# Linear attention and a ReLU MLP on one core: denominators computed per head, their reciprocals repeated through DRAM, and key sums on VectorE

## The chip, the cores and the metric

The kernel runs on one core of one Trainium2 chip. A core has five engines that run side by side and are held together by semaphores: TensorE (in the profile PE, with its weight loads as PEld), VectorE (DVE), ScalarE (ACT), GpSimd (POOL) and SyncE (SP), which here issues all DMA transfers. Operands lie in SBUF, a memory of 128 partitions; matmul results go to PSUM, eight banks of 128 x 512 fp32 values. The metric is the time of one execution on the device, in microseconds, as the median over runs.

## The reference

The input is x with 2048 rows of 512 bf16 values. The block is a linear attention with 32 heads of 16 values, followed by an MLP of width 1792, both behind a layer norm and a residual.

```
def _layernorm(x): return (x - mean(x)) / sqrt(var(x) + 1e-5)

def _A_ref(x, wqkv, wo):                     # H = 32, Dh = 16
    q, k, v = (x @ wqkv) split in three, by heads
    phi = lambda t: where(t > 0, t + 1, exp(t)) + 1e-6
    pq, pk = phi(q), phi(k)
    kv  = einsum("bhsd,bhse->bhde", pk, v)
    z   = einsum("bhsd->bhd", pk)
    num = einsum("bhqd,bhde->bhqe", pq, kv)
    den = einsum("bhqd,bhd->bhq", pq, z)[..., None] + 1e-6
    return (num / den, heads joined) @ wo

def _B_ref(x, w1, w2): return maximum(x @ w1, 0) @ w2

h   = x + _A_ref(_layernorm(x), wqkv, wo)
out = h + _B_ref(_layernorm(h), w1, w2)
```

The denominator is one number per row and head: a sum over the 16 features of the head, weighted by `z`, which is the sum of the key features over all 2048 rows.

## The kernel before

The 2048 rows are 16 tiles of 128 rows, and four tiles make a chunk of 512 rows. Nothing loops: a string ORDER lists every step as a word, and each engine carries out its own steps in the order in which the words stand. A word is a name and indices: `K.5.1` is step K of tile 5 into PSUM bank 1. Waits between engines follow from what the steps read and write. An engine that waits holds all its later steps, and SyncE's queue of DMA issues is such a queue too.

First stage, tile by tile. `lx` loads x; S and A take the statistics of the layer norm (VectorE), R their reciprocal root (ScalarE), N normalizes (VectorE). The result must be transposed: T and E (or V) do it on TensorE with a copy out of PSUM, X by a DMA that transposes on its way from SBUF to SBUF. K multiplies by the key weights; F (exp) and U (relu) on ScalarE and M (min, add) and D (add) on VectorE make the key features `pk` of the tile. G multiplies the normalized tile by `pk` and accumulates over all 16 tiles in four banks; from that, `gA` and `gD` (copy), `kv`, `kx` and `m` make the per-head product of keys and values, already multiplied by the output weights.

The sums `z` are matmuls as well: each of the four blocks of 128 features takes 16 matmuls, one per tile, with `pk` as weights and a single column of ones (line 337). `zc` copies the sums, `zh` lays them out in a mask by heads, 32 columns per block, and `zr` in a full mask of 128 columns, in which each of a head's 16 columns has the same weights.

Second stage, chunk by chunk. Q, qF, qU, qM, qD make the query features `pqT`, four blocks of 128 features by 512 rows. Then come the denominators, in two ways. In chunk 0, `d4` (line 386) makes four matmuls of 32 columns each, which write four quarters of one bank: one row per head. `dl4` and `dx4` take the logarithm and the exponential of its negative, which is the reciprocal, once for all blocks; `rp` (line 402) repeats each head's row over its 16 feature rows by a matmul with a 0/1 matrix `erep`, and `rm` (line 408) multiplies `pqT` by the result. In chunks 1 to 3, `d` (line 415) makes the denominators already repeated, a full matmul per block, and `dl`, `dx` and `dm` (lines 418, 423, 426) work on each block.

h (line 435) multiplies the scaled features by `m`, `hD` adds x, `s`, `a`, `n` are the second layer norm's statistics and subtraction, and the result is transposed again: tiles 0 to 3 on TensorE (`t`, with `e` or `v`), tiles 4 to 15 by DMA (`x`, line 270). `p` (line 450) multiplies by w1, `pA` (ScalarE) or `pD` (VectorE) take the relu out of PSUM, `f` (line 470) multiplies by w2, `fo` scales and adds the residual, `fd` stores. The last tile's `f` is done in two halves of 256 columns.

Of the kernel before, what the change touches and what calls it, by code (L numbers as in the profile page):

```python
# [18 lines left out]
table const masks warm.9.7 lx.0.1 S.0 lx.1.1 S.1 A.0 A.1 lx.2.2 S.3 S.2 R.1.1 R.0.1 lx.4.2 lk.0.2 lk.2.2  # L19
lx.6.2 A.3 A.2 N.0.2.2 N.0.0.2 N.1 R.2.2 N.2 N.3 warm.1.7 T.0.3.2.2 T.0.0.0.2 T.1.1 T.2.2 E.0.2.2 E.1 V.0.0.2  # L20
T.3.3 E.2 E.3 K.0.0 S.4 S.5 A.4 A.5 K.1.1 K.3.3 K.2.2 F.0.1 R.4.2 U.0.1 F.1.1 S.6 S.7 M.0.1 A.7 A.6 N.4 R.6.2
U.1.1 lx.8.4 T.4.0 D.0.1 G.0 M.1.1 N.5 N.7 T.5.1 E.4 U.2.1 F.2.1 E.5 F.3.1 U.3.1 K.4.0 D.1.1 S.9 N.6 S.8 G.1
M.2.1 A.9 A.8 D.2.1 R.8.2 K.5.1 F.4.2 U.4.2 M.3.1 S.10 N.8 D.3.1 N.9 M.4.2 S.11 D.4.2 lq.2.2 lq.0.2 lx.12.4
# [5 lines left out]
qF.0.2.2 qU.0.2.2 gD.0.2 z.0.2 z.2.2 z.3.2 zc qM.0.2.2 gA.2.2 zr zh qD.0.2.2 Q.1.1.3 Q.1.0.2 qF.1.0.2 qU.1.0.2
kv.1.4 kv.0.4 kv.2.4 kv.3.4 kx qM.1.0.2 Q.1.3.1 m.1.5 m.0.4 d4.0.3 m.3.7 m.2.6 Q.1.2.0 Q.2.0.2 dl4.0 mD.0.2  # L30
dx4.0 qU.1.2.2 qF.1.2.2 mD.2.2 rp.0.1.5 rp.0.2.6 rp.0.3.7 rp.0.0.4 Q.2.1.3 Q.2.3.1 Q.2.2.0 qU.2.0.2 qU.2.2.2
qF.2.0.2 qF.2.2.2 qD.1.0.2 rm.0.0.2 qM.1.2.2 rm.0.2.2 qD.1.2.2 h.1.5 h.0.4 hD.1 s.1 hD.0 h.3.7 Q.3.0.2 h.2.6
a.1 hD.3 n.1 t.1.5 Q.3.1.3 Q.3.2.0 Q.3.3.1 s.0 hD.2 s.3 s.2 a.0 a.3 a.2 n.0 e.1 n.3 t.0.4 t.3.7 n.2 v.3 t.2.6
# [15 lines left out]
f.8.4.0.7 f.8.4.7.7 fo.8 fd.8 x.15 f.9.5.0.7 f.11.7.0.7 f.11.7.7.7 f.10.6.0.7 p.3.3.3 f.9.5.7.7 p.3.2.2
p.3.1.1 p.3.0.0 pA.3.0.2 f.10.6.7.7 pD.3.2.2 p.3.4.0 p.3.5.1 p.3.6.2 p.3.7.3 fo.9 pA.3.4.2 p.3.9.1 fo.10 fo.11  # L50
pA.3.6.2 fd.9 fd.11 fd.10 p.3.8.0 f.12.4.0.7 pA.3.8.2 p.3.12.0 p.3.10.2 p.3.13.1 pA.3.12.2 r.12.4 p.3.11.3
pA.3.10.2 f.13.5.0.7 f.13.5.7.7 f.12.4.7.7 fo.12 fd.12 fo.13 fd.13 f.15.7.0.14.0.2 f.14.6.0.7 f.14.6.7.7
fo.15.0.2 fo.14 fd.15.0.2 fd.14 f.15.4.0.14.2.2 fo.15.2.2 fd.15.2.2
# [4 lines left out]
def kernel(  # L58
# [30 lines left out]
    big = ctx.enter_context(tc.tile_pool(name="big", bufs=1))  # L89
    psum = ctx.enter_context(tc.tile_pool(name="psum", bufs=1, space=bass.MemoryType.PSUM))  # L90
# [91 lines left out]

    def op_masks():
        nc.gpsimd.memset(mask[:], 1.0)
        keep(mask3, mask3, [[-DH, P // DH], [0, DH]], 0, 1)
        keep(mask3, mask3, [[DH, P // DH], [0, DH]], DH - 1, -1)
        nc.gpsimd.memset(mask_h[:], 1.0)
        keep(mask_h[:], mask_h[:], [[0, KD], [-DH, Q4]], 0, 1)
        keep(mask_h[:], mask_h[:], [[0, KD], [DH, Q4]], DH - 1, -1)
        nc.gpsimd.memset(erep[:], 1.0)  # L190
        for q in range(KD):
            rows = erep[q * Q4 : (q + 1) * Q4, :]
            keep(rows, rows, [[1, P]], 0, -DH)
            keep(rows, rows, [[-1, P]], DH - 1, DH)
# [139 lines left out]
    def op_z(jb, b):  # L334
        at_bank["z"] = b
        for t in range(NT):
            nc.tensor.matmul(  # L337
                bk[:, b, jb : jb + 1], lhsT=pk(t)[:, 0, jb * P : (jb + 1) * P], rhs=ones[:],
                start=(t == 0), stop=(t == NT - 1),
            )  # L340
# [55 lines left out]
    def op_dx4(c):  # L396
        nc.scalar.activation(out=rd[:, c % 2, :], in_=ld[:, c % 2, :], func=ACT.Exp, scale=-1.0)

    def op_rp(c, jb, b):
        at_bank["rp", c, jb] = b  # L400
        rows = slice(jb * Q4, (jb + 1) * Q4)
        nc.tensor.matmul(
            bk[:, b, :], lhsT=erep[rows, :], rhs=rd[rows, c % 2, :], start=True, stop=True
        )

    def op_rm(c, jb, n):
        i = (c * KD + jb) % NQ
        nc.vector.tensor_tensor(  # L408
            out=pqs[:, i : i + n, :], in0=bank(at_bank["rp", c, jb], n), in1=pqT[c][:, jb : jb + n, :],
            op=ALU.mult,  # L410
        )

    def op_d(c, jb, b):
        at_bank["d", c, jb] = b
        nc.tensor.matmul(bk[:, b, :], lhsT=zrep[:, jb, :], rhs=pqT[c][:, jb, :], start=True, stop=True)  # L415

    def op_dl(c, jb):
        nc.scalar.activation(  # L418
            out=ld[:, jb % 2, :], in_=bk[:, at_bank["d", c, jb], :], func=ACT.Ln, bias=eps6[:], scale=1.0
        )  # L420

    def op_dx(c, jb):
        nc.scalar.activation(out=rd[:, jb, :], in_=ld[:, jb % 2, :], func=ACT.Exp, scale=-1.0)

    def op_dm(c, jb):
        nc.vector.tensor_tensor(
            out=pqs[:, (c * KD + jb) % NQ, :], in0=pqT[c][:, jb, :], in1=rd[:, jb, :], op=ALU.mult
        )
# [92 lines left out]
```

## Time and profile before

| what | value |
|---|---|
| median of 3 runs | 174.51 us (174.10 to 175.42) |
| profiled execution, first to last instruction | 173.1 us; the page gives no other time for it |
| median above that span | 1.4 us |
| granted TensorE clock in that execution | 1.00 |
| DMA | 13.00 MB, mean 75 GB/s, issued by SyncE alone |
| TensorE's idle time between 22.83 and 170.06 us in the chain that ended last | none above 0.1 us at a time |
| issue of a DMA transpose on SyncE, and from issue to landing | 1.2 us, 2.4 us |
| issue of another DMA on SyncE | 0.33 to 0.58 us where its queue was not full |

How to read it: busy time of TensorE overlaps, since one matmul starts before the one ahead of it has left the array; what a step really takes is read from the chain that ended last, where consecutive starts are what counts. A line such as `L450` is a line of the kernel, and names like `bk<-lnT,w_sb` are written and read tiles: `bk` is PSUM, `gT` also serves as the output buffer, `at` holds the MLP's activations and, earlier, the key features of tiles 2 to 15. SPq is SyncE's queue of issues.

### The profile page before, as it was taken

The numbers are of one execution on the slowest core, as the hardware profiler recorded it, in microseconds if no ns is written. First come the engines' busy times: TensorE is split into PE (matmuls) and PEld (weight loads), VectorE is DVE, ScalarE is ACT, GpSimd is POOL, SyncE is SP. The second block draws the span as 40 slices with busy tenths as digits, with TensorE's granted clock in tenths as the row PEclk, the third lists the DMA queues.
The fourth block names the chain that finished last, engine by engine and source line by source line (L and its number), as shares of the span: only waits on it lengthen the run. The fifth ranks groups of instructions, "written<-read, shape, count | busy, mean of one in ns | idle before, by whom it ended". The sixth has DMA issues, their size and how long they took to land.

```text
span 173.1 us, 2263 instructions
## 1 busy us (share of the span) xinstructions
PE 165.8 (96%) x856; PEld 77.7 (45%) x872; DVE 99.7 (58%) x208; ACT 72.3 (42%) x112; POOL 4.7 (3%) x21
## 2 busy tenths in 40 slices
PE   7699989999999999999999999999999999999992
PEld 2244434446444544444444444444444444444551
DVE  3899965154799949796338089455769402500032
ACT  2499755666586794213057210006623000363100
POOL 7300000000000000000000000000000000000000
PEclk9999999999999999999999999999999999999999
DMA  5883456899000000002220000462001320010021
GB/s 139 280 307 61 77 132 152 255 364 360 4 0 0 4 0 0 0 0 61 61 64 30 0 2 0 108 78 91 0 0 30 65 60 0 30 62 0 0 80 45
DMA packets 19979, 13.00 MB, mean 75 GB/s; under 512 B 12544, under 2 KB 18816, under 8 KB 19968
## 3 DMA queue, kind: packets, MB, share of 16 engines
q1 hardware_dynamic: 19968, 12.85, 26.5%
q8 instruction: 7, 0.11, 0.3%
q14 instruction: 4, 0.03, 0.1%
HBM read 7.86 MB, written 2.10 MB: 58 GB/s over the span
## 4 chain that ended last, share of the span: by engine, by line
PE 85%; DVE 7%; DMA 5%; issue 1%; SPq 1%
PE bk L470 28%; PE bk L450 28%; PE bk L435 8%; PE bk L285 8%; PE bk L329 5%; PE bk L277 4%; DVE st L215 4%; DMA lnT<-h_nat 2%; DMA x_nat<-in_A_x_dram 2%; DVE h_nat L229 2%; PE bk L415 2%; PE bk L337 1%; DVE eb L302 1%; PE bk L374 1%; PE bk L248 1%
## 5 line engine op out<-in xcount | busy, mean ns | idle before, releaser
L450 PE MATMUL bk<-lnT,w_sb 128*128 128x512 bf16 x220 | 50.9, 379 | 0.2
L470 PE MATMUL bk<-w_sb,at 128*128 128x512 bf16 (+1 forms) x233 | 49.8, 366 | 0.3
L470 PEld LDWEIGHTS <-at 128*128 128x128 bf16 x238 | 23.3, 98 | 25.3
L450 PEld LDWEIGHTS <-w_sb 128*128 128x128 bf16 x224 | 21.9, 98 | 26.5
L456 ACT ACTIVATE at<-bk 128x1024 bf16<-128x1024 f32 x14 | 14.2, 1022 | 41.0 <-PE bk L450 22.3
L478 DVE SCALAR_TENSOR_TENSOR gT<-bk,rstd,h_nat 128x512 bf16<-128x512 f32 (+1 forms) x17 | 11.8, 716 | 30.4 <-PE bk L470 17.0
L461 DVE TENSOR_SCALAR at<-bk 128x1024 bf16<-128x1024 f32 x14 | 17.1, 1221 | 14.4 <-PE bk L450 14.4
L295 ACT ACTIVATE eb<-bk 128x1024 bf16<-128x1024 f32 (+1 forms) x18 | 16.6, 930 | 10.4 <-PE bk L277 6.1
L418 ACT ACTIVATE ld<-bk,eps 128x512 f32<-128x512 f32 x12 | 7.7, 693 | 27.7 <-PE bk L415 27.7
L298 ACT ACTIVATE rb<-bk 128x1024 bf16<-128x1024 f32 (+1 forms) x18 | 16.6, 927 | 1.3 <-DVE pqs L408 0.7
L277 PE MATMUL bk<-wk_sb,lnT 128*128 128x512 bf16 x64 | 15.3, 379 | 0.6 <-DMA lnT<-h_nat 0.6
L441 DVE TENSOR_TENSOR h_nat<-bk,x_nat 128x512 bf16<-128x512 f32 x16 | 10.7, 682 | 8.6 <-PE bk L435 8.6
L435 PE MATMUL bk<-m_sb,pqs 128*128 128x512 bf16 x62 | 15.2, 379 | 0.1
L285 PE MATMUL bk<-lnT,wq_sb 128*128 128x512 bf16 x61 | 14.7, 379 | 0.1
L329 PE MATMUL bk<-at,h_nat 128*128 128x512 bf16 x55 | 13.2, 379 | 0.1
L215 DVE BATCH_NORM_STATS2 st<-x_nat 128x6 f32<-128x512 bf16 x16 | 10.5, 680 | 2.7 <-DMA x_nat<-in_A_x_dram 2.7
L302 DVE TENSOR_SCALAR eb<-eb 128x1024 bf16<-128x1024 bf16 (+1 forms) x18 | 6.9, 389 | 7.0 <-ACT eb L295 7.0
L217 DVE BATCH_NORM_STATS2 st<-h_nat 128x6 f32<-128x512 bf16 x16 | 10.7, 683 | 0.2
L435 PEld LDWEIGHTS <-pqs 128*128 128x128 bf16 x64 | 6.3, 98 | 7.5
L277 PEld LDWEIGHTS <-lnT 128*128 128x128 bf16 x64 | 6.1, 98 | 7.9 <-DMA lnT<-h_nat 1.0
L329 PEld LDWEIGHTS <-h_nat 128*128 128x128 bf16 x64 | 6.2, 98 | 7.3
L285 PEld LDWEIGHTS <-wq_sb 128*128 128x128 bf16 x64 | 6.0, 98 | 6.9 <-issue 0.2
(63 smaller groups left out, 95.2 us busy)
## 6 DMA issues: line engine op xcount, KB each, us to landing
w_sb<-in_B_w_dram SPq DMA_DIRECT2D x4, 896.0 KB, 8.1
out_dram<-gT SPq DMA_DIRECT2D x15, 128.0 KB, 1.8
x_nat<-in_A_x_dram SPq DMA_DIRECT2D x2, 512.0 KB, 7.0
x_nat<-in_A_x_dram SPq DMA_DIRECT2D x3, 256.0 KB, 4.0
wk_sb<-in_A_wqkv_dram SPq DMA_DIRECT2D x2, 256.0 KB, 4.8
wq_sb<-in_A_wqkv_dram SPq DMA_DIRECT2D x2, 256.0 KB, 6.8
wv_sb<-in_A_wqkv_dram SPq DMA_DIRECT2D x2, 256.0 KB, 3.3
wo_sb<-in_A_wo_dram SPq DMA_DIRECT2D x2, 256.0 KB, 8.9
```

Of the source, the lines that this page charges most:

```text
L215: op_S = lambda t: nc.vector.bn_stats(out=st[:, t, :], in_=x_nat[:, t, :])
L277: nc.tensor.matmul(bk[:, b, :], lhsT=lnT[c][:, kd, j * P : (j + 1) * P], rhs=wk_sb[:, kd, :], start=(kd == 0), stop=(kd == KD - 1),)
L285: nc.tensor.matmul(bk[:, b, :], lhsT=wq_sb[:, kd, j * P : (j + 1) * P], rhs=lnT[c][:, kd, :], start=(kd == 0), stop=(kd == KD - 1),)
L295: nc.scalar.activation(out=buf(eb, kind, i, n), in_=bank(at_bank[kind, i], n), func=ACT.Exp)
L298: nc.scalar.activation(out=buf(rb, kind, i, n), in_=bank(at_bank[kind, i], n), func=ACT.Relu)
L329: nc.tensor.matmul(bk[:, KD + kd, :], lhsT=ln_nat[:, t, kd * P : (kd + 1) * P], rhs=pk(t)[:, 0, :], start=(t == 0), stop=(t == NT - 1),)
L435: nc.tensor.matmul(bk[:, b, :], lhsT=pqs[:, (c * KD + jb) % NQ, j * P : (j + 1) * P], rhs=m_sb[:, jb, :], start=(jb == 0), stop=(jb == KD ...
L450: nc.tensor.matmul(bk[:, b, :], lhsT=w1_sb[:, kd, f * P : (f + 1) * P], rhs=lnT[c][:, kd, :], start=(kd == 0), stop=(kd == KD - 1),)
L456: nc.scalar.activation(out=acts[c % 2][:, f : f + n, :], in_=bank(at_bank["p", c, f], n), func=ACT.Relu)
L461: nc.vector.tensor_scalar(out=acts[c % 2][:, f : f + n, :], in0=bank(at_bank["p", c, f], n), scalar1=0.0, scalar2=None, op0=ALU.max,)
L470: nc.tensor.matmul(bk[:, b, 0 : w * P], lhsT=acts[c % 2][:, f, j * P : (j + 1) * P], rhs=w2_sb[:, f, k * P : (k + w) * P], start=(f == 0), ...
L478: nc.vector.scalar_tensor_tensor(out=o_t[:, t % NO, cols], in0=bk[:, at_bank["f", t, k], 0 : w * P], scalar=rstd2[:, t : t + 1], in1=h_nat ...
```

## The change

Four things change, and ORDER is written anew around them.

1. Denominators by heads in all four chunks. `d4`, `dl4`, `dx4` are used for chunks 0 to 3. The reciprocals lie in `r4`, which takes over the SBUF of the key weights. `rw` writes them to a DRAM buffer `scr`, one DMA per block of 128 features: its source is 8 partitions (the block's 8 heads), each row of 512 read 16 times. `rr` reads two blocks back, 128 partitions each, into `rd`, which is one buffer for all chunks. `dm` multiplies two blocks at once. `rp`, `rm`, `d`, `dl`, `dx`, `zr`, `erep` and its masks go.
2. Key sums. `za` adds the key features of tiles 0 to 13, two tiles at a time and two columns of 512 beside each other, in fp32 on VectorE (six instructions of 1024 elements per partition); `zf` adds the two halves and splits the sum into a bf16 value and a bf16 rest. `z` then takes four matmuls per block: tiles 14, 15, value and rest.
3. Six more tiles go by DMA transpose: 4 and 5 in the first layer norm, 0 to 3 in the second.
4. Order: x is loaded tile by tile at first; a part of w2 is loaded in the middle of the MLP's first chunk; three G groups come after `z`; the denominators of chunks 2 and 3 stand earlier; 17 instead of 14 of the relu steps are on ScalarE; the last tile's `f` is in parts of 256, 128 and 128 columns.

```
+    r4 = wk_sb
+    z_acc = acts[1][:, 0:4, :].rearrange("p a n -> p (a n)").bitcast(F32).rearrange("p (a n) -> p a n", a=2)
+    scr = dram.tile([NCH, KD, P, CW], BF16, name="scr")
...
+    def op_za(t):
+        first = pk(0, 2) if t == 2 else z_acc
+        nc.vector.tensor_tensor(out=z_acc, in0=first, in1=pk(t, 2), op=ALU.add)
+
+    def op_zf(t):
+        z0, z1 = z_acc[:, 0, :], z_acc[:, 1, :]
+        nc.vector.tensor_tensor(out=z0, in0=z0, in1=z1, op=ALU.add)
+        nc.vector.tensor_copy(out=acts[1][:, 4, :], in_=z0)
+        nc.vector.tensor_tensor(out=acts[1][:, 5, :], in0=z0, in1=acts[1][:, 4, :], op=ALU.subtract)
...
+        parts = [pk(t)[:, 0, :] for t in range(t0, NT)] + [acts[1][:, i, :] for i in (4, 5) if t0]
+        for i, part in enumerate(parts):
+            nc.tensor.matmul(
+                bk[:, b, jb : jb + 1], lhsT=part[:, jb * P : (jb + 1) * P], rhs=ones[:],
+                start=(i == 0), stop=(i == len(parts) - 1),
             )
...
+        nc.scalar.activation(out=r4[:, c, :], in_=ld[:, c % 2, :], func=ACT.Exp, scale=-1.0)
+
+    def op_rw(c, jb):
+        src = r4[jb * Q4 : jb * Q4 + P // DH, c, :].rearrange("q (o n) -> q o n", o=1)
+        nc.sync.dma_start(
+            out=scr[c, jb].rearrange("(q r) n -> q r n", r=DH),
+            in_=src.broadcast_to([P // DH, DH, CW]),
+        )
+
+    def op_rr(c, jb, n):
+        nc.sync.dma_start(
+            out=rd[:, jb : jb + n, :], in_=scr[c, jb : jb + n].rearrange("j p n -> p j n")
+        )
+
+    def op_dm(c, jb, n=1):
         i = (c * KD + jb) % NQ
         nc.vector.tensor_tensor(
+            out=pqs[:, i : i + n, :], in0=pqT[c][:, jb : jb + n, :], in1=rd[:, jb : jb + n, :],
             op=ALU.mult,
```

The words of the new ORDER that the prediction walks through, from the last keys to the MLP:

```
... zf.12 D.14.2 G.11 G.12 qM.0.2.2 qU.0.2.2 z.2.2.14 z.1.2.14 z.0.2.14 z.3.2.14 l1.0.2 qM.0.0.2 qD.0.2.2
lv.0.2 G.13 zc qD.0.0.2 G.14 zh d4.0.1 lo.2.2 l1.2.2 dl4.0 lo.0.2 lv.2.2 G.15 Q.1.1.3 Q.1.0.2 dx4.0 gA.2.2
gD.0.2 kv.2.4 qF.1.0.2 qU.1.0.2 Q.1.3.1 Q.1.2.0 rw.0.0 kv.1.4 kv.0.4 kv.3.4 rw.0.1 rw.0.2 rw.0.3 qM.1.0.2
qF.1.2.2 rr.0.0.2 qD.1.0.2 kx Q.2.0.2 qU.1.2.2 m.0.4 m.3.7 m.2.6 m.1.5 qM.1.2.2 qD.1.2.2 mD.0.2 dm.0.0.2
rr.0.2.2 dm.0.2.2 mA.2.2 d4.1.0 dl4.1 Q.2.1.3 Q.2.3.1 h.3.6 h.2.7 hD.3 h.0.6 s.3 hD.2 dx4.1 rw.1.1 rw.1.0
rw.1.3 rw.1.2 rr.1.0.2 hD.0 s.2 a.3 s.0 Q.2.2.0 qU.2.0.2 qF.2.0.2 Q.3.0.2 h.1.4 Q.3.1.3 rr.1.2.2 qU.2.2.2 a.2
n.3 a.0 n.2 qF.2.2.2 x.3 hD.1 n.0 s.1 Q.3.2.0 Q.3.3.1 dm.1.0.2 x.2 x.0 dm.1.2.2 a.1 qM.2.0.2 n.1 h.5.7
qM.2.2.2 qD.2.0.2 qD.2.2.2 qU.3.0.2 h.4.5 h.7.6 qF.3.0.2 qF.3.2.2 qU.3.2.2 d4.2.1 h.6.4 x.1 p.0.0.2 ...
```

More of the change, by code (lines that the diff above doesn't have):

```diff
@@ L18 @@
 ORDER = """
[L19 to L23, printed above, removed]
@@ L29 @@
[L29 to L33, printed above, removed]
@@ L49 @@
[L49 to L53, printed above, removed]
+lx.1.1 const S.1 lx.0.1 S.0 lx.3.1 A.0 A.1 S.3 table warm.1.7 warm.9.7 lk.0.2 R.0.1 R.1.1 lx.2.1 N.0 A.3 R.3.1
@@ new lines @@
+T.0.4 N.1 lx.4.2 S.2 T.1.1 N.3 lk.2.2 E.0 E.1 A.2 S.4 lx.6.2 R.2.1 T.3.3 S.5 lx.8.4 K.0.6 A.4 A.5 N.2 E.3
+F.0.1 S.6 K.1.1 R.4.2 U.0.1 masks M.0.1 N.5 T.2.5 E.2 F.1.1 D.0.1 N.4 K.3.2 S.7 M.1.1 A.7 A.6 G.0 U.1.1
+lx.12.4 lq.0.2 D.1.1 X.5 S.8 K.2.3 R.6.2 N.6 G.1 X.4 F.2.1 U.2.1 F.3.1 X.6 K.5.1 S.9 A.8 M.2.1 A.9 N.7 R.8.2
+U.3.1 D.2.1 M.3.1 X.7 K.4.0 F.4.2 N.8 N.9 S.12 D.3.1 G.2 K.6.2 G.3 X.9 M.4.2 S.13 S.11 U.4.2 X.8 K.7.3 A.13
+A.12 R.12.2 K.9.1 D.4.2 S.10 A.11 l2.0.7 F.6.2 N.12 X.12 N.13 M.6.2 A.10 S.14 G.4 K.8.0 U.6.2 D.6.2 G.5 R.10.2
@@ new lines @@
+qM.2.2.2 qD.2.0.2 qD.2.2.2 qU.3.0.2 h.4.5 h.7.6 qF.3.0.2 qF.3.2.2 qU.3.2.2 d4.2.1 h.6.4 x.1 p.0.0.2 p.0.1.3
+dl4.2 qM.3.0.2 qM.3.2.2 hD.4 qD.3.2.2 hD.5 p.0.2.0 p.0.3.1 dx4.2 pA.0.0.2 rw.2.2 pA.0.2.2 s.5 a.5 hD.6
+qD.3.0.2 p.0.4.2 rw.2.0 rw.2.3 rw.2.1 rr.2.2.2 d4.3.4 p.0.5.3 p.0.6.0 p.0.7.1 hD.7 n.5 pA.0.4.2 p.0.9.3
+p.0.8.2 pD.0.6.2 pD.0.8.2 s.6 s.7 dl4.3 f.1.5.0.7 p.0.11.1 f.3.7.0.7 s.4 p.0.13.3 p.0.12.2 p.0.10.0 r.0.4
+dx4.3 pA.0.10.2 rr.2.0.2 dm.2.2.2 a.4 l2.7.7 rw.3.2 a.6 dm.2.0.2 a.7 n.7 n.4 h.8.6 rw.3.1 rw.3.0 x.5 rr.3.0.2
@@ new lines @@
+x.4 x.7 rw.3.3 f.0.4.0.7 n.6 pD.0.12.2 hD.8 h.9.6 h.10.3 x.6 rr.3.2.2 f.1.5.7.7 p.1.0.0 p.1.1.1 hD.10 dm.3.2.2
+r.4.4 pA.1.0.2 p.1.7.3 p.1.6.2 dm.3.0.2 pD.1.6.2 p.1.12.0 f.0.4.7.7 h.13.2 p.1.13.1 h.11.3 f.3.7.7.7 fo.0 s.8
+hD.13 hD.9 hD.11 pD.1.12.2 h.12.4 p.1.9.1 p.1.3.3 s.10 s.11 a.11 a.8 fo.1 p.1.2.2 s.9 fo.3 h.15.6 h.14.5
+p.1.8.0 hD.15 a.9 n.11 hD.12 pA.1.2.2 hD.14 pD.1.8.2 s.14 s.15 n.9 s.12 a.10 n.10 p.1.10.2 f.2.6.0.7 p.1.4.0
+f.2.6.7.7 p.1.5.1 pA.1.4.2 p.1.11.3 x.10 n.8 s.13 a.12 a.13 fo.2 pA.1.10.2 f.6.6.0.7 f.4.4.0.7 f.4.4.7.7
@@ new lines @@
+f.7.7.0.7 x.11 x.9 x.8 f.6.6.7.7 p.2.7.3 fd.3 fd.1 fd.2 p.2.5.1 p.2.4.0 p.2.6.2 pA.2.4.2 pD.2.6.2 f.7.7.7.7
+p.2.0.0 p.2.11.3 p.2.1.1 f.5.5.0.7 p.2.10.2 pA.2.0.2 a.14 a.15 n.13 n.12 pA.2.10.2 fd.0 n.15 n.14 fo.4 fo.6
+x.12 fd.4 x.14 p.2.9.1 p.2.8.0 p.2.3.3 f.5.5.7.7 p.2.2.2 pD.2.8.2 x.15 x.13 pD.2.2.2 fo.7 fo.5 fd.7 fd.5 fd.6
+p.2.13.1 p.2.12.0 r.8.4 pA.2.12.2 f.10.6.0.7 f.11.7.0.7 p.3.0.0 p.3.7.3 f.9.5.0.7 p.3.6.2 f.8.4.0.7 r.12.4
+p.3.1.1 pA.3.0.2 pD.3.6.2 f.9.5.7.7 f.8.4.7.7 p.3.13.1 p.3.2.2 p.3.12.0 f.10.6.7.7 p.3.3.3 f.11.7.7.7 fo.10
@@ L54 @@
+fo.11 fo.8 fo.9 pA.3.12.2 p.3.4.0 p.3.5.1 pA.3.2.2 pD.3.4.2 p.3.11.3 p.3.10.2 pA.3.10.2 p.3.9.1 p.3.8.0
+pA.3.8.2 f.12.4.0.7 f.15.7.0.14.0.2 f.13.5.0.7 f.13.5.7.7 f.12.4.7.7 fd.10 fd.11 fd.8 fd.9 fo.15.0.2 fo.13
+f.15.5.0.14.3.1 f.14.6.0.7 fo.15.3.1 fo.12 fd.12 fd.15.0.2 f.14.6.7.7 f.15.4.0.14.2.1 fo.14 fo.15.2.1
+fd.15.3.1 fd.13 fd.14 fd.15.2.1
 """
@@ L89 @@
     big = ctx.enter_context(tc.tile_pool(name="big", bufs=1))
+    dram = ctx.enter_context(tc.tile_pool(name="dram", bufs=1, space=bass.MemoryType.DRAM))
     psum = ctx.enter_context(tc.tile_pool(name="psum", bufs=1, space=bass.MemoryType.PSUM))
@@ L130 @@
     rstd = big.tile([P, NT], F32, name="rstd")
+    nmean = big.tile([P, NT], F32, name="nmean")
     st2 = big.tile([P, NT, nc.vector.BN_STATS_DIM], F32, name="st2")
@@ L189, in op_masks @@
         keep(mask_h[:], mask_h[:], [[0, KD], [DH, Q4]], DH - 1, -1)
[L190 to L194, printed above, removed]
     def op_lx(t, n):
@@ L222, in rstd_of, with op_ng, op_Np @@
         nc.scalar.activation(out=dst, in_=dst, func=ACT.Exp, scale=-0.5)
+    def op_ng(t, n):
+        nc.gpsimd.tensor_scalar(
+            out=nmean[:, t : t + n], in0=mv[:, t : t + n, 0], scalar1=-1.0, scalar2=None, op0=ALU.mult
+        )
+    def op_Np(t):
+        nc.gpsimd.tensor_scalar(
+            out=ln_nat[:, t, :], in0=x_nat[:, t, :],
+            scalar1=nmean[:, t : t + 1], scalar2=rstd[:, t : t + 1], op0=ALU.add, op1=ALU.mult,
+        )
     op_R = lambda t, n: rstd_of(rstd[:, t : t + n], mv[:, t : t + n, 1])
@@ L332, in op_G, with op_z @@
             )
-    def op_z(jb, b):
+    def op_za(t):
[6 more added lines that the diff above has]
+        nc.vector.tensor_tensor(out=acts[1][:, 5, :], in0=z0, in1=acts[1][:, 4, :], op=ALU.subtract)
+    def op_z(jb, b, t0=0):
         at_bank["z"] = b
-        for t in range(NT):
+        parts = [pk(t)[:, 0, :] for t in range(t0, NT)] + [acts[1][:, i, :] for i in (4, 5) if t0]
+        for i, part in enumerate(parts):
             nc.tensor.matmul(
-                bk[:, b, jb : jb + 1], lhsT=pk(t)[:, 0, jb * P : (jb + 1) * P], rhs=ones[:],
-                start=(t == 0), stop=(t == NT - 1),
+                bk[:, b, jb : jb + 1], lhsT=part[:, jb * P : (jb + 1) * P], rhs=ones[:],
+                start=(i == 0), stop=(i == len(parts) - 1),
             )
@@ L396, in op_dx4 @@
     def op_dx4(c):
[L397 to L403, printed above, removed]
-        )
-    def op_rm(c, jb, n):
+        nc.scalar.activation(out=r4[:, c, :], in_=ld[:, c % 2, :], func=ACT.Exp, scale=-1.0)
[4 more added lines that the diff above has]
+            in_=src.broadcast_to([P // DH, DH, CW]),
+        )
+    def op_rr(c, jb, n):
+        nc.sync.dma_start(
+            out=rd[:, jb : jb + n, :], in_=scr[c, jb : jb + n].rearrange("j p n -> p j n")
+        )
+    def op_dm(c, jb, n=1):
         i = (c * KD + jb) % NQ
         nc.vector.tensor_tensor(
-            out=pqs[:, i : i + n, :], in0=bank(at_bank["rp", c, jb], n), in1=pqT[c][:, jb : jb + n, :],
+            out=pqs[:, i : i + n, :], in0=pqT[c][:, jb : jb + n, :], in1=rd[:, jb : jb + n, :],
             op=ALU.mult,
[L411 to L427, printed above, removed]
         )
@@ L444, in op_hD, with op_p @@
         )
-    def op_p(c, f, b):
+    def op_p(c, f, b, s=0, n=1):
         at_bank["p", c, f] = b
+        cols = slice(s * CW // n, (s + 1) * CW // n)
         for kd in range(KD):
             nc.tensor.matmul(
-                bk[:, b, :], lhsT=w1_sb[:, kd, f * P : (f + 1) * P], rhs=lnT[c][:, kd, :],
+                bk[:, b, cols], lhsT=w1_sb[:, kd, f * P : (f + 1) * P], rhs=lnT[c][:, kd, cols],
                 start=(kd == 0), stop=(kd == KD - 1),
```

28 lines of the change are left out of this document (4 added, 24 removed).

## The prediction

> **What bounds the kernel now.** I read the shares of busy time first, then the busy table of stretches, then the chain that ended last in order of time, then the rows of the instructions that the change touches. Busy time, and TensorE and VectorE in 40 slices:
>
> ```profile
> PE 165.8 (96%) x856; PEld 77.7 (45%) x872; DVE 99.7 (58%) x208; ACT 72.3 (42%) x112; POOL 4.7 (3%) x21
> ...
> PE   7699989999999999999999999999999999999992
> PEld 2244434446444544444444444444444444444551
> DVE  3899965154799949796338089455769402500032
> ```
>
> TensorE (PE) is busy from end to end; VectorE (DVE) is full only in the opening. The stretches (us, then busy us of each engine) show that change-over:
>
> ```profile
> 8.70:22.80 14.10, 13.52 (x71) 6.25 (x69) 14.09 (x42) 12.01 (x27) 0.00 (x0) 1.00 0.52 152
> 22.80:42.50 19.70, 19.57 (x144) 9.78 (x146) 8.46 (x18) 12.94 (x15) 0.00 (x0) 1.00 0.84 254
> 42.50:61.00 18.50, 18.35 (x119) 8.85 (x118) 16.21 (x32) 12.83 (x15) 0.00 (x0) 1.00 0.04 14
> ```
>
> Before 22.8 us VectorE works 14.09 of 14.10 us; after it, 8.46 of 19.70. The chain (start, us, what) says what a step costs on TensorE, without the overlap that makes a single matmul look like 379 ns:
>
> ```profile
> 41.13 1.58 PE bk L337 x64
> 42.71 0.08 issue
> 42.79 1.67 PE bk L285 x7
> ...
> 46.75 0.33 PE bk L386 x4
> ...
> 49.34 0.33 PE bk L402 x4
> ...
> 59.52 0.67 PE bk L248 x12
> ...
> 117.35 0.43 PE bk L415 x2
> ...
> 170.09 0.48 DVE gT L478
> ```
>
> From 22.83 us to 170.06 the chain is matmuls without a gap worth naming. So the time falls by what TensorE no longer does, unless a new wait opens. A full matmul costs 0.216 us there, a group of four 0.86; a key-sum matmul 0.0247 (1.58/64); a transpose 0.056 (0.67/12); the four quarter-width denominators 0.33 together, as they overlap.
>
> **TensorE, removed and added.** Key sums: 48 of 64 go, 48 x 0.0247 = 1.2 us. The full-width denominators of chunks 1 to 3 (L415): 12 x 0.216 = 2.6. The repeat of chunk 0 (L402): 0.33. Four tiles of the second layer norm no longer transposed on TensorE: 16 x 0.056 = 0.9. Added: three more `d4` groups (L386), 3 x 0.33 = 1.0. Net 4.0 us. Tiles 4 and 5 of the first layer norm (8 transposes, 0.45) lie in the opening, where VectorE and loads decide; I count them at nothing. Span 173.1 - 4.0 = 169.1.
>
> **Opening.** Key weights still stand behind 768 KB of x in the queue, now as the seventh transfer instead of the sixth; they landed at about 8.4 us (issued at 3.1, 5.3 to landing), and the first K matmul ran at 8.7. The order of single tiles ahead of them gains nothing. GpSimd's repeat mask (2.7 us) goes, off the path. ScalarE loses 24 activations of 0.6 to 0.7 us and has room anyway.
>
> **Key sums on VectorE.** Nearest rows:
>
> ```profile
> L441 DVE TENSOR_TENSOR h_nat<-bk,x_nat 128x512 bf16<-128x512 f32 x16 | 10.7, 682 | 8.6 <-PE bk L435 8.6
> ...
> L305 DVE TENSOR_TENSOR pqT<-rb,eb 128x1024 bf16<-128x1024 bf16 x8 | 5.4, 679 | 0.0
> ...
> L408 DVE TENSOR_TENSOR pqs<-bk,pqT 128x1024 bf16<-128x1024 f32 x2 | 2.4, 1222 | 0.0
> ```
>
> Six `za` cost 4.1 us by the all-bf16 row and 7.3 by the row with an fp32 input; I take 7.3, as they read and write fp32. `zf` is 0.68 + 0.35 + 0.68 = 1.7. With 9.0 more, the stretch to 42.5 us holds 17.5 of 19.7: it fits, with little over. The tight place is the end: after K.15 TensorE has five groups (Q, G, Q, G, G: 4.3 us) before `z`, which now also needs D.14, and D.14 stands behind `zf` on VectorE. Its chain is F.14 1.02, M.14 0.43, `zf` 1.7, D.14 0.68, together 3.9. Fits by 0.4. After `z`, G.13 and G.14 (1.7) cover `zc` 0.16, one qD 0.68, `zh` 0.28. If `za` is late by some time, `z`, d4.0 and all behind them are late by it.
>
> **Reciprocals through DRAM.** No row of before shows a DMA that reads eight partitions sixteen times. Nearest are these (KB each, median us from issue to landing):
>
> ```profile
> out_dram<-gT SPq DMA_DIRECT2D x15, 128.0 KB, 1.8
> ...
> wv_sb<-in_A_wqkv_dram SPq DMA_DIRECT2D x2, 256.0 KB, 3.3
> ...
> lnT<-hn SPq DMA_TRANSPOSE x12, 2.4
> ```
>
> Chunk 0 is the tight one. Between the end of d4.0 and h.3, TensorE has G.15, seven Q groups, the value product (0.89), m (0.86) and d4.1: 0.86 + 6.05 + 0.89 + 0.86 + 0.33 = 9.0 us. Against it stand `dl4` 0.69, `dx4` 0.63, `dm` 0.68 and about 0.2 of hand-overs, which leaves 6.8 for the round trip. SyncE issues the four `rw` 0.45 apart and the last lands at 1.35 + 1.8 = 3.2; the last `rr` then lands 3.3 later, at 6.5. That just fits. But a 1 KB packet took 46 ns in the DMA records, a store spreads 128 of them over 16 engines, and a source of eight partitions may use eight: then each `rw` holds its engines 16 x 46 ns = 0.74 us, the last lands at 1.4 + 2.9 = 4.4 and the `rr` at 7.7, a stall of 0.9. The lower end is no stall, as an early landing gains nothing; the far end is the first rival, below. I take 0.4, between the two cases that stand nearest to the store's row. [...]
>
> `rr.0.0` waits on SyncE, and behind it stand the other `rr`, the four `rw` and two `rr` of chunk 1 and the transposes x.3, x.2, x.0, x.1, for which p.0 waits. At the taken price they are in time: d4.1 to h.5 has eleven groups, 9.5 us.
>
> **Between h.3 and p.0.** VectorE must do 4 residual adds, 4 statistics, 3 aggregates, 3 subtractions and both `dm` of chunk 1 before h.5. In before 4 of each kind took 6.3 us (53.3 to 59.6), so 5.9 and 1.36 for `dm`, 7.2; TensorE has eight groups after h.3, 6.9. Stall 0.3. The transpose of tile 1 by DMA costs 2.4 to landing instead of a TensorE pass: add 0.69, statistics 0.69, `dm` 1.36, aggregate 0.17, one qM 0.42, subtraction 0.35, 2.4: 6.1 us against 6.4 of cover (seven groups and d4.2). Hidden, by 0.3. Chunk 2 has 16 us of matmuls from d4.2 to h.8. Chunk 3's `rw` and `rr` stand between x.5 and x.6 on SyncE: VectorE reaches n.6 some 15 us after p.0.0 (its adds, statistics, evictions and `dm` summed as above), three queued transposes of 1.2 and a landing make 20, and TensorE has 21.1 before p.1.0 (14 p groups, 3 h groups, four half passes of 1.51, d4.3). No stall, with 1 over. The last tile in three parts ends in a smaller eviction, but its store is issued behind that of tile 14: nothing.
>
> **Sum.** 169.1 + 0.4 + 0.3 = 169.8 of span. The median run, 174.51, lies 1.4 above the profiled span of 173.1, so 171.2 us.
>
> **Rivals.** *Slower: the sixteen copies of a row are read one after the other.* All packets of before go to or from 128 partitions. If four neighbouring partitions share one reader, an `rw` takes 4 x 16 x 46 ns = 2.9 us instead of 0.4 to 0.7, and the four of a chunk, in one queue, 11.8. In chunk 0 the last lands at 13.2, its `rr` at 16.6: a stall of 9.8. The `rw` of chunk 1 wait on SyncE behind that `rr`, so h.5 is late by 6 more (13.8 + 1.4 + 11.8 + 3.4 + 0.7 = 31.1 against 17.3 + 7.8). 171.2 + 15.8 = 187. For it: 128 packets from eight rows. Against: nothing measured. With r us per `rw` the stalls are 4r - 2.1 in chunk 0 and 4r - 5.8 in chunk 1, so from r = 1.45 the 3.7 us that the rest of the change saves are used up, and past 1.65 the kernel is over 1% slower. [...]
>
> *About the same: the readers share by half, or VectorE is late with the key sums.* At 1.5 us per `rw` the last lands at 7.3, its `rr` at 10.7, a stall of 3.9: 174.7, and 0.2 more in chunk 1. `za` behind N.14 and N.15 by 2 us, which delays X.14, K.14 and `z`, gives 173.2.
>
> **Chances.** Forecast 0.55 (168.8 to 172.7); about the same 0.17 (172.7 to 176.3); slower 0.28 (up to 195, centre 187). One per cent, 1.75 us, is about what this kernel's measurement can tell from no change. The range leaves out 0.04 below 168.8 and the upper half of the slow case, so it reaches to 184.
>
> **What would show it.** Right: the chain without L415 and L402, `z` 0.4 us long, 157 to 160 us (161.4 before) between K.0's first matmul and the last, no wait of h.3 above 1 us. Wrong: TensorE idle before L435 (`h`) or L450 (`p`) with `rd` or SyncE behind it, `rw` landing over 3 us, or idle before the key sums with VectorE as releaser.

## The result: slower by a tenth, and the profile after

The changed kernel takes 193.74 us in the median of 4 runs (192.79 to 197.75), the kernel before 174.31 (173.97 to 175.42): a ratio of 1.108, with a 95% interval of 1.102 to 1.114. The forecast was 171.2, with a range up to 184. Its sign was wrong, and the time lies 10 us above the range.

The profiled execution of the changed kernel is the one of 197.75 us, with a span of 196.0; its mean granted clock was 0.948, against 0.956 to 0.964 in its other executions, so its waits are read here for their place and kind, and sizes are taken from other runs where that matters. Busy time, and TensorE and its granted clock in 40 slices:

```profile
PE 168.7 (86%) x795; PEld 75.4 (38%) x810; DVE 100.5 (51%) x203; ACT 64.3 (33%) x96; POOL 2.3 (1%) x12
...
PE   7599959999907939999940899999999999999993
...
PEclk9979999999985996999996699999999999999999
```

TensorE, full from end to end before, now has holes. Counted from 0, they stand at slice 5 in the opening, at slices 11 and 12, at slice 14, and at slices 20 and 21, the deepest. Behind the last three the granted clock went down to 0.50, for 6.83, 3.41 and 6.83 us; behind slice 5 it stayed at 1.00. From slice 23 on TensorE is dense as before. The waits (who waited for whom: us in total, times, longest) put names to the holes:

```profile
DVE pqs L430 <- DMA rd<-scr: 21.7, 5, 10.8
...
PE bk L440 <- DVE pqs L430: 10.0, 4, 5.4
...
PE bk L456 <- DMA lnT<-hn: 8.1, 1, 8.1
```

`h` (L440, L435 before) waits for the scaled features, these for the reciprocals read back from DRAM, and the first `p` of chunk 1 (L456, L450 before) for a transpose. The chain that ended last, before one row of matmuls, now leaves TensorE three times after its first matmuls (start, us, what; single lines of it):

```profile
22.18 6.05 DMA lnT<-h_nat
...
43.55 0.36 PE bk L403 x4
43.90 0.02 issue
43.93 0.69 ACT ld L409
...
44.65 0.64 ACT wk_sb L414
...
45.30 0.85 SPq L418
...
48.73 8.72 DMA scr<-wk_sb
...
57.96 0.69 SPq L418
...
61.37 8.81 DMA scr<-wk_sb
...
70.23 2.96 DMA rd<-scr
...
91.95 8.19 DMA scr<-wk_sb
...
104.05 4.31 DMA lnT<-hn
...
108.49 1.86 PE bk L456 x4
```

L418 is `rw`, the write of the reciprocals. Four of them were issued from 45.30 us on, and the last had landed at 57.45: 12.2 us, where the forecast had 3.2 to 4.4. The second set starts at 57.96, when SyncE has at last issued the read of the first, and takes as long. The last lines are chunk 3, where a transpose is held up behind the same writes. In the DMA records the 1 KB packets of chunk 0's writes took 140 ns in the median and 147 at the 90th percentile, against a median of 46 in the profile of before, and mostly six to eight of them were under way at a time, which I read as eight engines. With 16 on each of them and four writes in one queue, 64 x 0.14 is 9 us, and it is 10.7 if the 1.4 us from the issue to the first packet (45.30 to 46.75 us) are taken off the 12.2: 2.3 to 2.7 us per `rw`.

### The profile page after: what moved, and what is told of

It is laid out like the page before. It is cut to its first block, busy times and chain, and to the rows that moved or that the text cites. A ratio compares the mean times of both kernels' runs of the same rounds, so it can differ in the third digit from the quotient of the medians.

```text
span 196.0 us, 2153 instructions
## 1 busy us (share of the span) xinstructions
PE 168.7 (86%) x795; PEld 75.4 (38%) x810; DVE 100.5 (51%) x203; ACT 64.3 (33%) x96; POOL 2.3 (1%) x12
## 4 chain that ended last, share of the span: by engine, by line
PE 55%; DMA 26%; SPq 9%; DVE 4%; issue 2%; ACT 2%
PE bk L476 21%; PE bk L456 19%; DMA scr<-wk_sb 16%; SPq L418 6%; PE bk L440 4%; PE bk L286 4%; PE bk L338 3%; DMA lnT<-h_nat 3%; DMA wk_sb<-in_A_wqkv_dram 3%; DMA lnT<-hn 2%; DVE st L213 2%; PE bk L294 2%; DMA rd<-scr 2%; SPq L279 1%; SPq L196 1%
## 5 line engine op out<-in xcount | busy, mean ns | idle before, releaser
L456 PE MATMUL bk<-lnT,w_sb 128*128 128x512 bf16 x218 | 52.4, 386 | 8.6 <-DMA lnT<-hn 8.1
L476 PE MATMUL bk<-w_sb,at 128*128 128x512 bf16 (+2 forms) x248 | 51.0, 355 | 0.2
L462 ACT ACTIVATE at<-bk 128x1024 bf16<-128x1024 f32 x17 | 17.3, 1023 | 82.2 <-PE bk L456 82.2
L456 PEld LDWEIGHTS <-w_sb 128*128 128x128 bf16 x224 | 22.1, 99 | 35.9 <-issue 10.7
L467 DVE TENSOR_SCALAR at<-bk 128x1024 bf16<-128x1024 f32 x11 | 13.4, 1222 | 32.1 <-PE bk L456 27.0
L440 PE MATMUL bk<-m_sb,pqs 128*128 128x512 bf16 x63 | 19.2, 444 | 10.0 <-DVE pqs L430 10.0
L484 DVE SCALAR_TENSOR_TENSOR gT<-bk,rstd,h_nat 128x512 bf16<-128x512 f32 (+2 forms) x18 | 11.9, 684 | 22.3 <-PE bk L476 22.2
L286 PE MATMUL bk<-wk_sb,lnT 128*128 128x512 bf16 x63 | 16.9, 405 | 3.6 <-DMA lnT<-h_nat 1.9
L430 DVE TENSOR_TENSOR pqs<-pqT,rd 128x1024 bf16<-128x1024 bf16 x8 | 5.4, 684 | 21.7 <-DMA rd<-scr 21.7
L440 PEld LDWEIGHTS <-pqs 128*128 128x128 bf16 x64 | 6.6, 110 | 21.2 <-DVE pqs L430 12.4
L338 PE MATMUL bk<-at,h_nat 128*128 128x512 bf16 x56 | 13.7, 380 | 0.1
L286 PEld LDWEIGHTS <-lnT 128*128 128x128 bf16 x64 | 6.4, 102 | 11.7 <-issue 3.1
```

The source lines that it names most:

```text
L286: nc.tensor.matmul(bk[:, b, :], lhsT=lnT[c][:, kd, j * P : (j + 1) * P], rhs=wk_sb[:, kd, :], start=(kd == 0), stop=(kd == KD - 1),)
L338: nc.tensor.matmul(bk[:, KD + kd, :], lhsT=ln_nat[:, t, kd * P : (kd + 1) * P], rhs=pk(t)[:, 0, :], start=(t == 0), stop=(t == NT - 1),)
L440: nc.tensor.matmul(bk[:, b, :], lhsT=pqs[:, (c * KD + jb) % NQ, j * P : (j + 1) * P], rhs=m_sb[:, jb, :], start=(jb == 0), stop=(jb == KD ...
L456: nc.tensor.matmul(bk[:, b, cols], lhsT=w1_sb[:, kd, f * P : (f + 1) * P], rhs=lnT[c][:, kd, cols], start=(kd == 0), stop=(kd == KD - 1),)
L462: nc.scalar.activation(out=acts[c % 2][:, f : f + n, :], in_=bank(at_bank["p", c, f], n), func=ACT.Relu)
L467: nc.vector.tensor_scalar(out=acts[c % 2][:, f : f + n, :], in0=bank(at_bank["p", c, f], n), scalar1=0.0, scalar2=None, op0=ALU.max,)
```

## The experiments

The theory after this profile (A): packets that read neighbouring partitions wait for each other. The rival (B): eight source rows or eight engines are too few, or the way through DRAM is slow in itself. A time below is a median, with its range in brackets, or that of a single execution; the kernel before took 175.7 us on each of the two chips of these runs, 1.4 more than in the result above.

### Rows four partitions apart

The denominator matmul has 32 columns per block and uses 8. The mask is changed so that each head fills four neighbouring columns, and `rw` reads every fourth row.

```
-        keep(mask_h[:], mask_h[:], [[0, KD], [-DH, Q4]], 0, 1)
-        keep(mask_h[:], mask_h[:], [[0, KD], [DH, Q4]], DH - 1, -1)
+        keep(mask4, mask4, [[0, KD], [-DH, P // DH], [0, 4]], 0, 1)          # mask4: mask_h as (8 heads, 4)
+        keep(mask4, mask4, [[0, KD], [DH, P // DH], [0, 4]], DH - 1, -1)
...
-        src = r4[jb * Q4 : jb * Q4 + P // DH, c, :]
+        src = r4[jb * Q4 : (jb + 1) * Q4 : 4, c, :]
```

> Only the rows change from which rw reads: each block's eight heads stand four partitions apart (the head mask gives each head four neighbouring columns of the denominator matmul, and rw reads every fourth row) instead of in eight neighbouring partitions. Bytes, packets (128 of 1 KB), the sixteen readings of one row, the number of source rows and so of engines (eight) stay. Theory A, neighbouring partitions share one reader: a packet of rw goes from about 140 ns back to 46 to 60, an rw takes 0.7 to 1 us, the stalls before h.3, h.5 and p.1 shrink from 18 us together to under 4, and the time is 170 to 175. Theory B, eight source rows or eight engines are too few, or the way through DRAM is slow in itself: packets stay at 140 ns and the time within 3 us of 193.

Measured: 172.26 and 177.40 us. The profile is of the second, whose granted clock was at 0.50 for 6.8 us in the opening, long before any `rw`. The packets of `rw` took 46 ns in the median, and 46 at the 90th percentile too; mostly seven to nine were under way at a time, so the engines are no more than before. What is left of the wait for the reciprocals:

```profile
DVE pqs L430 <- DMA rd<-scr: 3.9, 3, 1.8
```

Nothing changed but the distance of the rows: same bytes, same number of rows, same repetition, same way through DRAM. B falls with that, in all its forms. TensorE waits 0.74 and 1.00 us at h.3; its other waits for the reciprocals are gone, and with them 20 us of time.

### All 32 rows of a block

```
-        src = r4[jb * Q4 : jb * Q4 + P // DH, c, :]
-        out=scr[c, jb].rearrange("(q r) n -> q r n", r=DH), in_=src.broadcast_to([P // DH, DH, CW])
+        src = r4[jb * Q4 : (jb + 1) * Q4, c, :]
+        out=scr[c, jb].rearrange("(q r) n -> q r n", r=4), in_=src.broadcast_to([Q4, 4, CW])
```

> As the kernel with rows four apart, but each rw reads all 32 rows of its block, each four times. Theory A: packets at 46 ns, as there; little left to gain over the rows four apart, within 2 us of it (169 to 174). Theory B, the count of rows or engines decides: this one is fast (170 to 174) while the one with eight rows four apart stays at 193.

Measured: 172.17 and 173.37 us, a ratio of 0.983 to before (0.977 to 0.990). A `rw` lands in 2.4 us. The time is as A has it, the packets are not: those of chunk 0's writes took 71 ns in the median and 79 at the 90th percentile, where A expected 46. These rows are neighbours again, and mostly 13 to 16 packets are under way at a time, which I read as sixteen engines. If four neighbouring partitions share one reader, as the prediction's rival has it, that is two packets on each such four, where rows four apart put one. It costs nothing that the time shows (172.17 us, against 172.26), since twice the engines share the work: by these packets an `rw` takes 8 x 71 ns = 0.57 us, against 16 x 46 ns = 0.74, as an estimate.

### Rows two partitions apart

```
+        src = r4[jb * Q4 : jb * Q4 + 16 : 2, c, :]      # each head in two neighbouring columns
```

> The changed kernel with the eight rows of a block two partitions apart instead of neighbours (each head has two columns of the denominator matmul, rw reads every second of 16 rows). Theory, four neighbouring partitions share one reader: two rows on a reader instead of four, so packets at half of 140 ns, about 70 to 75, an rw at 1.2 us, waits for the reciprocals of 1 to 4 us in all and a time of 173 to 177. If it is a matter of exactly neighbouring rows: 46 ns as with four apart, 172. If of eight partitions or engines in all: 140 ns, 193.

Measured: 176.70 and 179.17 us, a ratio of 1.0145 (1.005 to 1.024). In the stretch of chunk 0's writes the packets took 69 ns in the median and 79 at the 90th percentile. The size of the step is as A says, half of 140. TensorE's waits in its timeline (of the execution of 179.17 us) are 1.03 and 0.86 us at h.3 and 2.01 before `p`, 3.9 together. That is the upper end of what was expected, and the time reaches past it: this execution's first key matmuls also ran at half the granted clock (6 in 2.56 us, against 1.46 at full clock).

The three together, with the change itself (packets of chunk 0's writes, median and 90th percentile):

| rows of a block | packets at a time on four neighbouring partitions, estimated from those under way | packet of `rw`, ns | time, us (shortest) |
|---|---|---|---|
| 8 neighbours | 4 | 140, 147 | 192.8 to 193.0 |
| 8, two apart | 2 | 69, 79 | 176.7 |
| 32 neighbours, sixteen engines | 2 | 71, 79 | 172.2 |
| 8, four apart | 1 | 46, 46 | 172.3 |

140 ns is three times 46 and not four. An estimate that fits the four rows of the table takes 46 ns a packet as the pace of one engine and 35 (140/4) as that of four neighbouring partitions together: two packets on such a group then take 70 each (69 and 71 measured), and one takes 46, where the engine is the slower of the two.

A group may hold more than four neighbours. In all four profiles with eight neighbouring rows, about half of the packets took under 60 ns for some 1 us where chunk 0's second write hands over to the third (51.25 to 52.25 us in the first profile of the change), and none did where the first hands over to the second. The first two writes read partitions 0 to 7 and 32 to 39, the other two 64 to 71 and 96 to 103. So rows 32 apart seem to wait for each other and rows 64 apart not; no run tests it.

### One write for a chunk, and the w2 load moved

One DMA reads all 128 rows, each four times, instead of four that read eight; the head mask is that of rows four apart. The load of the first half of w2, which in the change stands ahead of the transposes of tiles 12 and on in SyncE's queue, goes behind that of tile 15.

```
-rw.0.0 ... rw.0.1 rw.0.2 rw.0.3
+rw.0
...
-A.11 l2.0.7 F.6.2 N.12 X.12
+A.11 F.6.2 N.12 X.12 ... X.15 l2.0.7
...
+        src = r4[:, c, :]
+        out=scr[c].rearrange("j (q r) n -> (j q) r n", r=4), in_=src.broadcast_to([P, 4, CW])
```

> Two edits: the four rw of a chunk are one DMA over all 128 partitions, each row read four times; and the first half of w2 (896 KB) is loaded behind the transpose of tile 15 instead of ahead of that of tile 12. Theory A: no packet over 60 ns, no stall above 1 us before h.3, h.5, p.1. Theory on the opening: the 4.4 us for which TensorE waits for the transpose of tile 12 is the load ahead of it in the queue; it goes, and the time is 166 to 171, faster than before. If the wait has another cause (VectorE with the key sums), it stays, and the time is 171 to 175.

Measured: 171.16 us (171.15 to 171.22), a ratio of 0.974 to before (0.970 to 0.978): faster than both kernels, and 0.2 us above what was expected. The packets of the writes took 46 to 48 ns in the median in chunks 1 and 2, and the waits for the transpose of tile 12 and at h.3, h.5 and p.1 are gone. The page and the chain of this kernel:

```profile
PE   7779999999999999999999999999999999999992
...
scr<-wk_sb SPq DMA_DIRECT2D x4, 512.0 KB, 3.3
rd<-scr SPq DMA_DIRECT2D x8, 256.0 KB, 2.8
```

```profile
38.48 0.38 PE bk L357 x16
38.86 1.75 PE bk L338 x8
40.61 0.33 PE bk L403 x4
...
48.73 1.83 PE bk L294 x8
50.56 2.31 PE bk L440 x10
```

The 512 KB of a chunk's reciprocals land in 3.3 us, and `h` follows the last Q group without a wait. Chunk 0's way of 6.1 us (3.3 + 2.8) is inside the 6.8 that the prediction left for it.

### The w2 load alone

```
-A.11 l2.0.7 F.6.2 N.12 X.12
+A.11 F.6.2 N.12 X.12 ... X.15 l2.0.7
```

> The changed kernel with one word moved: the load of the first half of w2 stands behind the transpose of tile 15 instead of ahead of that of tile 12. The reciprocals' way is as in the change. Theory: the load ahead in the queue holds the transposes and with them the key matmuls of tile 12, 4.4 us of TensorE's idle time that nothing later gives back; the time falls by 3 to 5 us, to 188 to 190. Rival, the key sums on VectorE hold the opening, or the wait is hidden by the later waits for the reciprocals: it stays within 1.5 us of 193.

Measured: 191.45 and 192.19 us, 1 us below the change's shortest, 192.79 and 192.97 (the latter under "The change once more"), so the time sides with the rival. The trace shows what the load had cost: the wait for the transpose of tile 12 is gone, and d4 of chunk 0 starts at 39.8 us, where the change had it at 43.5 and 43.9 in its two profiles. Those are executions of 197.75 and 195.92 us, and in both the granted clock was at 0.50 for 3.4 us of the opening. The kernel with filler in the holes, the next one, has the change's opening; in its execution of 191.03 us at a granted clock of 1.00, d4 starts at 42.2, and its timeline has this wait (L290 there is the key matmul, L286 in the change):

```profile
27.01 2.76 PE L290 MATMUL bk<-wk_sb,lnT 128*128 128x512 bf16 x11 [1.94 <-DMA lnT<-h_nat]
```

So the load costs some 2 us of the opening at full clock, and not 4.4. This kernel and the one before it differ in the reciprocals' write alone, which makes it the place to count the loss. TensorE's waits (start, us, what, in brackets the idle time before it):

```profile
55.29 1.03 PE L440 MATMUL bk<-m_sb,pqs 128*128 128x512 bf16 x2 [4.88 <-DVE pqs L430]
57.40 4.02 PE L440 MATMUL bk<-m_sb,pqs 128*128 128x512 bf16 x9 [1.08 <-DVE pqs L430]
...
67.37 0.61 PE L440 MATMUL bk<-m_sb,pqs 128*128 128x512 bf16 x2 [0.77 <-DVE pqs L430]
69.73 2.33 PE L440 MATMUL bk<-m_sb,pqs 128*128 128x512 bf16 x10 [1.75 <-DVE pqs L430]
...
102.14 1.87 PE L456 MATMUL bk<-lnT,w_sb 128*128 128x512 bf16 x4 [7.62 <-DMA lnT<-hn]
104.22 3.90 PE L456 MATMUL bk<-lnT,w_sb 128*128 128x512 bf16 x15 [0.22 <-issue]
```

The waits are 6.0 at h.3, 2.5 at h.5 and 7.6 before p.1, 16.1 together. Behind them matmuls run slowly: 9 in 4.02 us instead of 2.1, 4 in 1.87 and a pause instead of 1.0, 15 in 3.90 instead of 3.4, about 3.5. With 0.4 of a wait for the value weights that is 20.0, against a difference of the two spans of 189.7 - 169.5 = 20.2 us.

### TensorE kept busy in the holes

```
+    def op_wm(n, b):      # n matmuls whose result is not used
+        for _ in range(n):
+            nc.tensor.matmul(bk[:, b, :], lhsT=wq_sb[:, 0, 0:P], rhs=wq_sb[:, 0, :], start=True, stop=True)
...
+wm.24.6 h.3.6 ... wm.16.7 h.5.7 ... wm.34.0 p.1.0.0
```

> The changed kernel with 24, 16 and 34 matmuls that write nothing of use, put into TensorE's queue where it idles: before h.3, before h.5 and before p.1.0. The waits are as they were. Theory: after an idle stretch TensorE works at a lower granted clock for some microseconds, which is 5 to 7 us of the loss beside the idle time itself; then the time falls to 186 to 189. If the loss is idle time alone, it stays at 192 to 194, or rises where the fillers overrun a gap.

Measured: 191.03 and 191.22 us, a ratio of 1.088 (1.082 to 1.094). The granted clock is 1.00 throughout, and the matmuls behind the wait are quick (L444 is `h`):

```profile
59.50 2.48 PE L444 MATMUL bk<-m_sb,pqs 128*128 128x512 bf16 x10 [1.36 <-DVE pqs L434]
```

Ten matmuls of `h` in 2.48 us, where 9 took 4.02. But the time fell by 1.8 us only, not by 5 to 7: my estimate was too large, taken from the profile of 197.75 us. From d4 of chunk 0 to the end of the span this execution takes 147.1 us and that with the w2 load alone 149.9, so behind the opening the filler is worth 2.8, nearer to the 3.5 counted there. The lower clock is the smaller part of the loss (2.8 to 3.5 us), the waits are the larger (16.1).

### The key sums back on TensorE

```
-z.2.2.14 ... za.2 za.4 za.6 za.8 za.10 za.12 zf.12
+z.2.2 ...
```

> The kernel with one write per chunk and the moved w2 load, with the key sums back on TensorE: za and zf are left out, z takes all 64 matmuls. Theory of the sum: TensorE does 48 more matmuls of 0.0247 us, so the time is 171.2 + 1.2 = 172.4 (172.0 to 172.7). Rival: the 9 us of additions on VectorE cost the opening as much as they save; then 171.2 or less.

Measured: 171.82 us (171.63 to 174.78), a ratio of 0.979 (0.974 to 0.984), against 171.16 with the sums on VectorE. The two ran on different chips. By their shortest times the move is worth 0.5 us, by their ratios to the kernel before 0.9, and TensorE's count gives 1.2. Where the rest goes was not tried; with the sums on VectorE, VectorE is busy for 30.79 of the 33.5 us from 9.0 to 42.5, nearly as long as TensorE with 32.90.

### The order of the first loads

```
-lx.1.1 lx.0.1 lx.3.1 lk.0.2 lx.2.1 lx.4.2 lk.2.2
+lx.1.1 lx.0.1 lk.0.2 lk.2.2 lx.3.1 lx.2.1 lx.4.2      # keys first
+lx.1.1 lx.0.1 lx.3.1 lk.0.2 lx.2.1 lk.2.2 lx.4.2      # with the filler
```

> The kernel with one write per chunk and the moved w2 load, with both halves of the key weights loaded behind the first two tiles of x, ahead of tiles 2 to 5. In it TensorE waits from 7.8 to 9.3 us for the key weights. Theory, that wait is on the path: K.0 starts 1 to 2 us earlier and the time falls by 0.5 to 1.5, to 169.7 to 170.7. Rival, the opening is VectorE's, which gets tiles 2 to 5 later: 171 to 172.

> As the kernel with the filler, and the second half of the key weights loaded ahead of tiles 4 and 5 of x (not ahead of tiles 2 and 3). Theory: the first K matmul starts 0.5 to 1 us earlier and tiles 4 and 5 are not late on VectorE, so the time is 0.3 to 0.8 below that of the filler alone. Rival: as with both halves ahead of tiles 2 to 5, VectorE gets its tiles later, and the time is 171.2 to 172.

Measured: 172.72 us (172.56 to 172.92) with both halves of the key weights first, 172.74 (171.56 to 173.44) with one half and the filler below. Both are slower than without the edit, and above the 172 that the rivals gave as well. TensorE no longer waits for the weights but for normalized tiles:

```profile
PE bk L257 <- DVE h_nat L238: 2.5, 2, 1.9
```

The line is of the kernel with both halves first; its granted clock was also at 0.50 for 3.4 us in the opening. With one half and the filler the clock was 1.00, the wait 2.3, and d4 of chunk 0 came at 42.2 us, against 40.5 without either edit. So the rivals have the cause right: in these two orders it is VectorE's chain from x to the normalized tile that TensorE waits for in the opening, 2.5 and 2.3 us.

### Filler in the opening

```
-T.1.1 ... T.3.3
+T.1.1 warm.3.7 ... T.3.3 warm.7.7
```

> The kernel with one write per chunk and the moved w2 load, and ten more matmuls of no use between the first transposes, where TensorE waits for the key weights until about 9.3 us. Theory: the granted clock sags in that wait in some executions, so that the first K matmuls take twice their time; with the filler they never do, and the time is 170.6 to 171.3 with a narrow spread. If the sag costs nothing on the path (VectorE holds the opening), the time stays at 171.2.

Measured: 171.48 us (171.30 to 171.76), a ratio of 0.975 (0.971 to 0.980): no gain over 171.16, and d4 of chunk 0 starts at 40.5 us in both profiles. What the sag costs is not shown by this run, since the granted clock was 1.00 in all four executions of the kernel without the filler. The profile of rows four apart says more: its clock sagged for 6.8 us, and its d4 came at 44.6 us, against 41.3 in that of all 32 rows, which has the same opening and full clock. Of these 3.3 us, 1.5 are key weights that landed later; the rest goes with the slower matmuls, so a sag can cost time where it happens.

### The change once more

> The changed kernel as it is, for a second look at its waits. Theory: TensorE's waits are those of the first profile (about 6.5 us before h.3, 3.5 before h.5, 8 before p.1.0), the time is 192 to 194, and the granted clock, lower in the first profile for a longer time after each wait, accounts for the rest of the difference between the two.

Measured: 192.97 and 195.92 us; the profile is of the second. The waits are 5.42 and 0.78 us at h.3, 1.03 and 1.33 at h.5, 7.32 before p.1, and in the opening 2.26 for the key weights and 1.52 for a transpose. The places are those of the first profile. That one had the granted clock at 0.50 for one stretch of 3.4 us more, at h.5, where ten matmuls of `h` took 3.99 us against 2.33 here.

## Why the prediction was wrong, point by point

**The step that failed** is the price of `rw` under "Reciprocals through DRAM". It took 46 ns for a packet, and asked only how many engines share the work: 0.4 to 0.7 us per `rw`, a stall of 0.4. A packet took 140 ns, an `rw` 2.3 to 2.7 us, and TensorE waited 6.0 us at h.3 (with the w2 load alone). Nothing in the profile of before spoke against that, as all its packets go to or from 128 partitions; the rows taken as nearest were the wrong kind of near, alike in bytes and not in where they read. The engine count, which the prediction weighed instead, made no difference to the time: eight engines (seven to nine packets under way) gave 172.26 us, sixteen (13 to 16) 172.17.

**The rival that came true** was the slower one, by its mechanism: rows four apart bring the packets back to 46 ns. Its place was right too, h.3, then the `rw` of chunk 1 on SyncE behind the `rr` of chunk 0. Its price was 2.9 us per `rw`, measured 2.3 to 2.7. With r = 2.6 its formula gives 8.3 and 4.6 us in chunks 0 and 1; measured were 6.0 and 2.5 of TensorE's idle time. It gave 187 in all and was still short of 193, for two reasons. It counted no wait in chunk 3, where I had seen the `rw` stand between x.5 and x.6 and found 1 us over at the low price, and did not go back to that place with the high one: that wait is the longest, 7.6. And it left out the slow matmuls after each wait.

**The chance** of 0.28 for that rival was too low for what was known: the prediction named that 128 packets come from eight rows, and gave "nothing measured" as the reason against. The range, too, ended at 184, below the 187 that the prediction itself gave as the centre of that case.

**The sum** for TensorE held. With the reciprocals' write spread out and the w2 load moved, the time is 171.16, against 171.2 forecast. That near an agreement is luck in part: the kernel before took 175.75 us in the same runs, so the gain is 4.6 us where 3.3 were forecast. Within it, `z` takes 0.38 us (0.4 forecast), three of the four `d4` groups 0.33 each and the second 0.66. `za` took 1.22 us each, 7.3 together, as taken. The stalls of 0.4 at h.3 and 0.3 before h.5 did not come, and the key sums gave 0.5 to 0.9 instead of 1.2, errors that cancel in part. "Hidden" for the transposes of tiles 0 to 3, with 0.3 over, was right: p.0 follows without a wait there.

**The opening** was wrong in two places. It gives the first half of w2 no price: I did not see that the new order moves its load ahead of the transposes of tiles 12, 13, 11 and 10: a transpose then landed 6.05 us after its issue instead of 2.4. It shows as a wait of TensorE in both profiles of the change, and it is gone when the load is moved, for a gain of 1 us in time. And the key weights, as the seventh transfer, were not there when TensorE came for their second half: it waited 0.9 to 2.3 us for them in the profiles of the change, of the w2 load alone and of the fastest kernel, where I had counted no change. Loading them first gained nothing.

**What stays open:** why of some 2 us in the opening the moved w2 load gives only 1 in time, why the key sums give less than their count, what a sag of the clock in the opening costs, and whether rows 32 partitions apart wait for each other.

## What to carry to other kernels

Ask of every small DMA not only how many bytes and engines, but from which partitions it reads: here a packet took 140 ns from eight neighbouring rows and 46 from eight that are four apart. So a row that is read over and over wants its copies spread over the partitions, which here cost nothing, as a matmul had idle columns to put them in (with four columns per head, three of the four `d4` groups took 0.33 us, as in the kernel before). When a queue of issues holds a wait, price everything that stands behind it at the high end of the unknown too, down to the last place where the same steps occur. And when an order is written anew, look at each bulk load for the small transfers that it now stands ahead of.

## What the runs showed that I had not expected

- The pace of the reciprocals' writes went with the distance of the rows that they read, in steps: with eight rows and eight engines, 140, 69 and 46 ns for 1 KB at one, two and four partitions apart; with sixteen engines on 32 neighbouring rows, 71.
- After waits of 4.9 and 7.6 us TensorE's matmuls were slow: with the w2 load alone, four took 1.87 us instead of 1.0. The granted clock was at 0.50 there for 6.83 us, and in other places for 3.41. How long a wait has to be was not shown: once one of 2.01 us was enough (rows two apart, before `p`), and waits of 0.77 and 1.75 us at h.5 were not (w2 load alone). Matmuls of no use in the gaps kept the clock at 1.00.
- Issuing an `rw` from eight rows held SyncE for 0.67 to 0.85 us, and up to 2.95 for the third and fourth of a set, against 0.52 to 0.61 for the single write of 128 rows.
